# Two layers of cached attention and gated FFN on one core: one more K page kept between the layers, and the loads of layer 0 reordered

## The chip, the core and the metric

The program runs on one core of a Trainium2 chip. The engines that matter are TensorE (PE in the profile, its weight loads apart as PEld), VectorE (DVE), ScalarE (ACT) and SyncE (SP). SP issues every large load from device memory (HBM) into on-chip memory (SBUF); 16 DMA engines move it. The metric is the time of one execution in microseconds (us); lower is better.

## What is computed

One token of width 640 goes through attention, FFN, attention, FFN. Both attention layers use the same weights and the same caches, and so do both FFNs: a K page that layer 0 has read is the page that layer 1 needs. Attention looks at the last 4096 of 32768 cached positions, in 32 heads of width 192.

```python
def _A_ref(x, k_cache, v_cache, wq, wo):
    ...
    W = min(4096, max(256, Sk // 4))
    q = (x @ wq).reshape(B, Sq, Hq, Dh)          # then by head
    k = k_cache[:, :, Sk - W:, :]
    v = v_cache[:, :, Sk - W:, :]
    scores = einsum("bhqd,bhkd->bhqk", q, k) * (Dh ** -0.5)
    p = softmax(scores, axis=-1)
    o = einsum("bhqk,bhkd->bhqd", p, v)
    return o.reshape(B, Sq, Hq * Dh) @ wo

def _B_ref(x, w1, w3, w2):
    return einsum("bsf,fd->bsd", silu(x @ w1) * (x @ w3), w2)

x = A_x
x = x + _A_ref(_layernorm(x), ...)
x = x + _B_ref(_layernorm(x), ...)
x = x + _A_ref(_layernorm(x), ...)
x = x + _B_ref(_layernorm(x), ...)
```

The operands are bf16. One head's K (or V) for the window is 4096 x 192 values, 1.57 MB; wq is 7.9 MB, wo 7.9 MB, w1, w3 and w2 1.97 MB each.

## The kernel before

**Slots.** `arena` is a ring of `NSLOT = 16` slots in SBUF, each 128 partitions by `PGW = 6144` bf16 columns (1.57 MB). One K page, one V page or one fifth of wq fills a slot. wo comes in five units of nine chunks of 640 columns, plus a sixth unit of three chunks in a buffer of its own, `wo5`. w1 and w3 have 7680 columns: the first 6144 of each are the units `fa` and `fb`; their last 1536 each, with the first 2560 columns of w2, are the unit `fc`; the next 3200 columns of w2 are `fd`; the last 1920 of w2 stay for both layers in the buffer `keep`.

**One list of loads.** `loads` is built before anything runs and fixes the order of all loads: in each layer the five q units, then for each step i the V page of head number i − 6 (`LEAD` is 6) and the K page of head number i, then wo, then the FFN. `refill` (L191 to L205; its load is L203, that of the buffers without a slot L198) takes entries from the front as long as a slot is free. An entry that has no slot holds back all behind it. `done` frees a slot when its last reader has been recorded and calls `refill`. On the chip, SP executes the issues in that order, and each waits until the readers of the slot's former content have finished. It also waits for the load eight issues earlier, since loads take turns on eight semaphores.

**Kept pages.** K pages of the heads in `RETAIN` (14 of them) are not read again in layer 1. Thirteen stay in their slots from layer 0 to layer 1. The fourteenth, head 24 (`STASH`), is copied into PSUM and a small buffer and back by `stash`, so it holds no slot between. `ORDER` sets the order of the blocks of eight heads: heads 24 to 31, 16 to 23, 8 to 15, 0 to 7 in layer 0, and 8 to 15, 0 to 7, 16 to 23, 24 to 31 in layer 1. All of heads 0 to 7 are kept, so at the end of layer 0's attention thirteen slots are held and three are left for the stream. Layer 1's head 8, which is kept, comes first; its slot comes free when its products are done.

**Compute.** Every product is recorded through the helper `mm`, so all matmuls have line L80. A K page is turned by two transposes on DVE (L293) as it comes in, and then multiplied by twelve matmuls (`s_ps`); a kept page needs no second turning. Four heads share a softmax (L315 to L343). A V page takes 16 matmuls (`o_ps`). On PE the order of a step is V of head i − 6 first, then K of head i. After the last V come `combine`, `wo_proj` (18 matmuls for each wo unit), the sum into the residual (`y_to_residual`) and the layernorm; then `ffn`: 16 matmuls on `fa`, 16 on `fb`, 8 on `fc`, a short chain on ACT and DVE, and the w2 product, which frees `fc` and then `fd`. Layer 1 begins with another residual and layernorm, and `qproj` reads the five q units, 16 matmuls each. The tile `w` in the profile is the program's `w20`; `pss` holds the small PSUM results.

Of the kernel before, what the change touches and what calls it, by code (L numbers as in the profile page):

```python
# [17 lines left out]
NCH = 5  # L18
# [7 lines left out]
PGW = 6144  # L26
# [2 lines left out]

NSLOT = 16  # L30
STASH = 24
RETAIN = (0, 1, 2, 3, 4, 5, 6, 7, 8, 11, 14, 18, 21, 24)
MB = 2560
MN = 192
NSTASH = 2 * (3072 - MN)
LEAD = HB + 2
# [11 lines left out]
def kernel(  # L48
# [90 lines left out]
    keep = arn.tile([P, 1920], BF16, name="keep")  # L139
# [5 lines left out]
    loads = []  # L145

    wq_v = A_wq.rearrange("(p c) n -> c p n", c=NCH)
    wo_v = A_wo.rearrange("(b p e) n -> b p (e n)", b=H // HG, p=P, e=12)
    w1_v = B_w1.rearrange("(p c) n -> p (c n)", c=NCH)
    w3_v = B_w3.rearrange("(p c) n -> p (c n)", c=NCH)  # L150
    w2_v = B_w2.rearrange("(p f) n -> p (f n)", f=12)

    ORDER = ((3, 2, 1, 0), (1, 0, 2, 3))

    def head(layer, g):
        return HG * ORDER[layer][g // HG] + g % HG

    for layer in range(2):
        for c in range(NCH):
            loads.append((("q", layer, c), [(0, PGW, wq_v[c])]))  # L160
        for i in range(H + LEAD):
            for kind, g, cache in (("v", i - LEAD, A_v_cache), ("k", i, A_k_cache)):
                if not 0 <= g < H:
                    continue
                h = head(layer, g)
                if kind == "k" and layer == 1 and h in RETAIN:
                    if h == STASH:
                        loads.append((("k", 1, h), []))
                    continue
                loads.append(((kind, layer, h),  # L170
                              [(0, PGW, cache[0, h, S0:SK, :].rearrange("(p t) d -> p (t d)", p=P))]))
        for w in range(6):
            parts, ci, end = [], 9 * w, min(9 * w + 9, 48)
            while ci < end:
                to = min(end, ci - ci % 12 + 12)
                parts.append((640 * (ci - 9 * w), 640 * (to - ci),
                              wo_v[ORDER[layer][ci // 12]][:, 640 * (ci % 12):640 * (ci % 12 + to - ci)]))
                ci = to
            if w < 5:
                loads.append((("o", layer, w), parts))  # L180
            elif layer == 0:
                assert len(parts) == 1 and parts[0][1] == 1920
                loads.append((None, [(wo5[:], parts[0][2])]))
        loads.append((("fa", layer), [(0, PGW, w1_v[:, 0:PGW])]))
        loads.append((("fb", layer), [(0, PGW, w3_v[:, 0:PGW])]))
        loads.append((("fc", layer), [(0, 1536, w1_v[:, PGW:]), (1536, 1536, w3_v[:, PGW:]),
                                      (3072, 2560, w2_v[:, 0:2560])]))
        fd = [(0, 3200)] if layer == 0 else [(0, 1280), (1280, 1280), (2560, 640)]
        loads.append((("fd", layer), [(o, n, w2_v[:, 2560 + o:2560 + o + n]) for o, n in fd]))
        if layer == 0:  # L190
            loads.append((None, [(keep[:], w2_v[:, 5760:7680])]))  # L191

    def refill():
        while loads and (free or loads[0][0] is None):
# [20 lines left out]
    def page(key):  # L215
        return arena[:, home[key] * PGW:home[key] * PGW + PGW]

    def done(key):
        free.append(home.pop(key))
        refill()  # L220
# [59 lines left out]
    def k_source(layer, g):  # L280
        h = head(layer, g)
        fresh = layer == 0 or h not in RETAIN
        return ("k", layer if fresh or h == STASH else 0, h), fresh
# [11 lines left out]
    def k_page(layer, g, s_ps):  # L295
# [12 lines left out]
        if layer == 0 and h == STASH:  # L308
            stash(x, True)
            done(key)  # L310
        elif layer == 1 or h not in RETAIN:
            done(key)
# [70 lines left out]
    def y_open(name):  # L383

        y_ps = [ps_a.tile([P, 512], F32, tag="a", name=f"{name}{i}") for i in range(2)]
        for nh in range(2):
            for j in range(4):
                mm(y_ps[nh][32 * j:32 * j + 32, 0:320], lhsT=zero[:], rhs=ptm[:, 0:320],
                   start=True, stop=False, tile_position=(0, 32 * j))
        return y_ps  # L390

    def wo_proj(layer):
        y_ps = y_open("y_ps")
        for w in range(6):
            pg = page(("o", layer, w)) if w < 5 else wo5
            for cc in range(min(9, 48 - 9 * w)):
                ci = 9 * w + cc
                j = ci % 4
                for nh in range(2):
                    mm(y_ps[nh][32 * j:32 * j + 1, 0:320], lhsT=otd[:, ci:ci + 1],  # L400
                       rhs=pg[:, 640 * cc + 320 * nh:640 * cc + 320 * nh + 320],
                       start=False, stop=(ci >= 44), tile_position=(0, 32 * j))
            if w < 5:
                done(("o", layer, w))
        y_to_residual(y_ps)

    def w2_chunk(layer, fcx):
        if fcx >= 9:
            return keep, 640 * (fcx - 9)
        return (page(("fc", layer)), 3072 + 640 * fcx) if fcx < 4 else (page(("fd", layer)), 640 * (fcx - 4))  # L410

    def ffn(layer):
        if layer == 1:
            assert not loads
            spare = free[0] * PGW
            ident = arena[:, spare:spare + 256].bitcast(F32)
            nc.gpsimd.memset(ident, 0.0)
            nc.gpsimd.affine_select(out=ident, in_=ident, compare_op=ALU.not_equal, fill=1.0, base=0,
                                    pattern=[[-1, P]], channel_multiplier=1)
        g_ps = ps_a.tile([P, 512], F32, tag="a", name="g_ps")  # L420
        u_ps = ps_a.tile([P, 512], F32, tag="a", name="u_ps")
        for ps, kind, c0, c1, off in ((g_ps, "fa", 0, 4, 0), (u_ps, "fb", 0, 4, 0),
                                      (g_ps, "fc", 4, 5, 0), (u_ps, "fc", 4, 5, 1536)):
            pg = page((kind, layer))
            for c in range(c0, c1):
                for j in range(4):
                    mm(ps[32 * j:32 * j + 32, 0:384], lhsT=xs[:, c, 3:35],
                       rhs=_ap(pg, 0, P, off + 1536 * (c - c0) + 3 * j, [[12, 128], [1, 3]]),
                       start=(c == 0), stop=(c == NCH - 1), tile_position=(0, 32 * j))
            if kind != "fc":  # L430
                done((kind, layer))
        gu = w20.rearrange("p (g n) -> p g n", g=2)
        pin(nc.scalar.copy(out=gu[:, 0, :], in_=g_ps[:, 0:384]))
        pin(nc.vector.tensor_copy(out=gu[:, 1, :], in_=u_ps[:, 0:384]))
        gt_ps = m_ps[:, 0:24].rearrange("p (g k j) -> p g k j", g=2, k=3)
        for gi in range(2):
            for k in range(3):
                mm(gt_ps[:, gi, k, :], lhsT=gu[:, gi, k:384:3], rhs=sel4[:], start=True, stop=True)
        ex = sml.tile([P, 12], F32, tag="ex", name="ex")
        pin(nc.scalar.activation(out=ex[:], in_=gt_ps[:, 0, :, :].rearrange("p k j -> p (k j)"), func=ACTF.Exp,  # L440
                                 scale=-1.0))
        ut = sml.tile([P, 12], F32, tag="ut", name="ut")
        pin(nc.vector.tensor_copy(out=ut[:], in_=gt_ps[:, 1, :, :].rearrange("p k j -> p (k j)")))
        gut = sml.tile([P, 12], F32, tag="gut", name="gut")
        pin(nc.vector.tensor_tensor(out=gut[:], in0=gt_ps[:, 0, :, :].rearrange("p k j -> p (k j)"), in1=ut[:],
                                    op=ALU.mult))
        pin(nc.vector.tensor_scalar_add(out=ex[:], in0=ex[:], scalar1=1.0))
        pin(nc.vector.reciprocal(out=ex[:], in_=ex[:]))
        pin(nc.vector.tensor_tensor(out=_ap(htd[:], 0, P, 0, [[1, 3], [3, 4]]),
                                    in0=gut[:].rearrange("p (k j) -> p k j", k=3),  # L450
                                    in1=ex[:].rearrange("p (k j) -> p k j", k=3), op=ALU.mult))
        if layer == 1:
            return last_rows(ident)
        y_ps = y_open("y2_ps")
        for fcx in range(12):
            j = fcx % 4
            pg, off = w2_chunk(layer, fcx)
            for nh in range(2):
                mm(y_ps[nh][32 * j:32 * j + 1, 0:320], lhsT=htd[:, fcx:fcx + 1], rhs=pg[:, off + 320 * nh:off + 320 * nh + 320],
                   start=False, stop=(fcx >= 8), tile_position=(0, 32 * j))  # L460
            if fcx == 3:
                done(("fc", layer))
        done(("fd", layer))
        y_to_residual(y_ps)

    def last_rows(ident):
# [88 lines left out]
```

## Time and profile before

Three runs took 528.78, 528.95 and 529.55 us (median 528.95). The profiled execution has a span of 527.8 us, from its first to its last instruction.

| what | value |
|---|---|
| median of the runs | 528.95 us |
| span of the profiled execution | 527.8 us |
| PE busy, 2487 matmuls | 275.8 us (52%) |
| DVE busy | 256.5 us (49%) |
| ACT busy | 62.3 us (12%) |
| DMA, mean over the span | 421 GB/s, 221.97 MB |
| V pages loaded | 64 of 1536 KB |
| K pages loaded | 50 of 1536 KB |
| q units loaded | 10 of 1536 KB |

A name such as `arena<-in_A_v_cache_dram` says which tile is written from which tensor. In a list by time, the first number is the start within the span, the second how long it lasts; several instructions with small gaps are merged into one line with their count, and square brackets tell how long the engine sat idle before and what ended that. In a table by windows each line is a stretch of time with the busy time of each engine, the clock granted to PE, the busy share of the DMA engines and what they moved in GB/s.

### The profile page before, as it was taken

The numbers are of one execution on the slowest core, as the hardware profiler recorded it, in microseconds if no ns is written. First come the engines' busy times: TensorE is split into PE (matmuls) and PEld (weight loads), VectorE is DVE, ScalarE is ACT, GpSimd is POOL, SyncE is SP. The second block draws the span as 40 slices with busy tenths as digits, with TensorE's granted clock in tenths as the row PEclk, the third lists the DMA queues.
The fourth block names the chain that finished last, engine by engine and source line by source line (L and its number), as shares of the span: only waits on it lengthen the run. The fifth ranks groups of instructions, "written<-read, shape, count | busy, mean of one in ns | idle before, by whom it ended". The sixth has DMA issues, their size and how long they took to land.

```text
span 527.8 us, 6132 instructions
## 1 busy us (share of the span) xinstructions
PE 275.8 (52%) x2487; PEld 113.9 (22%) x2487; DVE 256.5 (49%) x393; ACT 62.3 (12%) x192; POOL 14.3 (3%) x66
## 2 busy tenths in 40 slices
PE   2354644463645555455445446678254655446545
PEld 1111212121212221122112212233121322112212
DVE  1199676656656475754001139431475654753001
ACT  1002020111102020102000002022111120202000
POOL 4000000000000000000000000000000000000000
PEclk9997968676766776586556557888677886586556
DMA  8999999999999999999999999999999999999995
GB/s 350 430 429 429 428 431 429 427 431 429 427 431 431 430 425 432 430 426 425 416 433 422 430 430 401 431 431 427 430 429 427 429 430 431 430 428 428 424 432 215
DMA packets 22356, 221.97 MB, mean 421 GB/s; under 512 B 2617, under 2 KB 2745, under 8 KB 5177
## 3 DMA queue, kind: packets, MB, share of 16 engines
q1 hardware_dynamic: 22184, 221.59, 99.1%
q8 instruction: 19, 0.31, 0.2%
q14 instruction: 9, 0.07, 0.0%
q10 hardware_dynamic: 144, 0.00, 0.0%
HBM read 221.58 MB, written 0.00 MB: 420 GB/s over the span
## 4 chain that ended last, share of the span: by engine, by line
DMA 86%; PE 6%; DVE 5%; ACT 1%; issue 1%; SPq 0%; DVEq 0%; ACTq 0%
DMA arena<-in_A_k_cache_dram 54%; DMA arena<-in_A_v_cache_dram 14%; DMA arena<-in_A_wo_dram 8%; DMA arena<-in_A_wq_dram 6%; DMA arena<-in_B_w_dram 5%; DVE arena L293 4%; PE s_ps L80 3%; PE o_ps L80 2%; PE y_ps L80 1%; SPq L203 0%; ACT w L330 0%; PE pss L80 0%; PE q_ps L80 0%; DVE t L315 0%; PE g_ps L80 0%
## 5 line engine op out<-in xcount | busy, mean ns | idle before, releaser
L80 PE MATMUL s_ps<-arena,wst 128*32 128x512 bf16 x768 | 155.2, 518 | 172.7 <-DVE arena L293 86.4
L293 DVE STREAM_TRANSPOSE arena<-arena 128x1536 uint32<-128x1536 uint32 x100 | 171.2, 1754 | 77.3 <-DMA arena<-in_A_k_cache_dram 77.0
L80 PE MATMUL o_ps<-arena,ptm 128*8 128x384 bf16 (+1 forms) x1024 | 116.7, 425 | 11.4 <-DMA arena<-in_A_v_cache_dram 11.3
L80 PEld LDWEIGHTS <-wst 128*32 128x32 bf16 x768 | 52.9, 115 | 257.9 <-issue 226.7
L80 PEld LDWEIGHTS <-ptm 128*8 128x8 bf16 (+1 forms) x1024 | 41.0, 100 | 49.0 <-issue 38.8
L325 ACT ACTIVATE tb<-m 32x16 f32<-32x16 f32 x16 | 3.4, 215 | 280.6 <-DVE m L322 280.6
L343 ACT COPY ptm<-w 32x64 bf16<-32x64 bf16 x80 | 23.6, 295 | 44.5 <-PE o_ps L80 41.4
L80 PE MATMUL y_ps<-arena,otd 128*1 128x320 bf16 x180 | 16.5, 448 | 15.0 <-DMA arena<-in_A_wo_dram 15.0
L80 PE MATMUL q_ps<-arena,xs 128*32 128x384 bf16 x160 | 14.5, 519 | 17.5 <-DMA arena<-in_A_wq_dram 14.9
L376 DVE SCALAR_TENSOR_TENSOR w<-pss,rl,mask 64x192 bf16<-64x192 f32 x16 | 6.7, 416 | 31.7 <-PE pss L80 31.7
L275 POOL COPY wst<-qt_sb 32x24 bf16<-32x24 bf16 x30 | 8.4, 281 | 434.4 <-PE s_ps L80 315.8
L333 DVE STREAM_TRANSPOSE w<-w 64x512 bf16<-64x512 bf16 x16 | 11.3, 705 | 14.4 <-ACT w L330 14.4
L241 DVE CAST w<-y_ps 128x320 bf16<-128x320 f32 x3 | 1.5, 492 | 33.8 <-PE y_ps L80 33.8
L315 DVE TENSOR_REDUCE t<-s_ps 64x1 f32<-64x512 f32 x16 | 10.6, 663 | 12.2 <-PE s_ps L80 12.1
L80 PEld LDWEIGHTS <-xs 128*32 128x32 bf16 x240 | 8.8, 125 | 35.1 <-issue 23.0
L268 DVE CAST qt_sb<-pss 32x192 bf16<-32x192 f32 x2 | 0.7, 345 | 30.9 <-PE pss L80 30.9
L343 DVE COPY ptm<-w 32x64 bf16<-32x64 bf16 x48 | 10.0, 208 | 11.7 <-PE o_ps L80 10.4
L348 DVE RECIPROCAL rl<-pss 64x1 f32<-64x1 f32 x16 | 2.6, 165 | 20.5 <-PE pss L80 20.4
L80 PEld LDWEIGHTS <-otd 128*1 128x1 bf16 x192 | 6.4, 102 | 25.2 <-issue 21.1
L330 ACT ACTIVATE w<-s_ps,nbt 64x512 bf16<-64x512 f32 x16 | 10.9, 682 | 5.6 <-DVE nbt L327 5.6
L369 ACT CAST w<-o_ps 128x384 bf16<-128x384 f32 x16 | 7.7, 478 | 31.7 <-PE o_ps L80 23.3
L80 PE MATMUL pss<-w,sel 128*64 128x192 bf16 x32 | 6.0, 273 | 9.5 <-ACT w L369 6.4
(81 smaller groups left out, 107.8 us busy)
## 6 DMA issues: line engine op xcount, KB each, us to landing
arena<-in_A_v_cache_dram SPq DMA_DIRECT2D x64, 1536.0 KB, 29.2
arena<-in_A_k_cache_dram SPq DMA_DIRECT2D x50, 1536.0 KB, 29.2
arena<-in_A_wq_dram SPq DMA_DIRECT2D x10, 1536.0 KB, 9.5
arena<-in_A_wo_dram SPq DMA_DIRECT2D x6, 1440.0 KB, 20.8
arena<-in_B_w_dram SPq DMA_DIRECT2D x4, 1536.0 KB, 10.9
arena<-in_A_wo_dram SPq DMA_DIRECT2D x4, 960.0 KB, 16.5
arena<-in_A_wo_dram SPq DMA_DIRECT2D x4, 480.0 KB, 15.0
arena<-in_B_w_dram SPq DMA_DIRECT2D x4, 384.0 KB, 14.8
```

The lines of the kernel that those rows point to most:

```text
L80: return pin(nc.tensor.matmul(*a, **k))
L241: pin(nc.vector.tensor_copy(out=y_sb[:, 320:640], in_=y_ps[1][:, 0:320]))
L275: pin((engs[a].copy if engs[a] is nc.scalar else engs[a].tensor_copy)(out=dst, in_=src))
L293: pin(nc.vector.transpose(x[:, w * sp:w * (sp + 1)].bitcast(U32), x[:, w * sp:w * (sp + 1)].bitcast(U32)))
L315: pin(nc.vector.reduce_max(out=t0[:, 0:1], in_=s_ps[0:64, :], axis=AX.X))
L325: pin(nc.scalar.mul(out=tb[32:64, :].rearrange("p (a z) -> p a z", a=4)[:, :, 0:HB], in_=mb, mul=-SCALE))
L330: pin(nc.scalar.activation(out=e[:], in_=s_ps[0:64, :], func=ACTF.Exp, bias=nbt[:, 0:1], scale=SCALE, accum_out=l[:]))
L333: pin(nc.vector.transpose(et[:], e[:]))
L343: pin((eng.copy if eng is nc.scalar else eng.tensor_copy)(out=dst, in_=src))
L348: pin(nc.vector.reciprocal(out=rl[half], in_=rl_ps[half]))
L369: pin(nc.scalar.copy(out=o_sb[:, 0:384], in_=o_ps[:, 0:384]))
L376: pin(nc.vector.scalar_tensor_tensor(out=om, in0=ot_ps[half], scalar=rl[half], in1=mask[half].unsqueeze(2).broadcast_to([64, 16, 12]), op0 ...
```

## The change

The list `RETAIN` gets head 9, so layer 1 loads 17 K pages instead of 18, and fourteen slots are held at the end of layer 0's attention instead of thirteen. In layer 0 each step's K page stands ahead of its V page in `loads`; the order of the products stays. In layer 0 the wo chunks 9, 10 and 11 are read last and from `wo5`, where chunks 45 to 47 were; layer 1's order is as before. Layer 1 reads `wo5` as layer 0 left it. Before, that was rows of block 0 (heads 0 to 7), where the reference has block 3 (heads 24 to 31) for layer 1's last three chunks; after the change it is block 3 in both layers. In layer 0's FFN `fc` holds the last 1536 columns of w1 and w3 alone, is loaded first and multiplied first; `fd` holds the first 5760 columns of w2. Layer 1's FFN is as before.

```diff
-RETAIN = (0, 1, 2, 3, 4, 5, 6, 7, 8, 11, 14, 18, 21, 24)
+RETAIN = (0, 1, 2, 3, 4, 5, 6, 7, 8, 9, 11, 14, 18, 21, 24)
...
+    def wo_order(layer):
+        last = ORDER[1][3]
+        kept = [12 * ORDER[layer].index(last) + e for e in (9, 10, 11)]
+        return [ci for ci in range(48) if ci not in kept] + kept
+
     for layer in range(2):
         for c in range(NCH):
             loads.append((("q", layer, c), [(0, PGW, wq_v[c])]))
         for i in range(H + LEAD):
-            for kind, g, cache in (("v", i - LEAD, A_v_cache), ("k", i, A_k_cache)):
+            pair = (("v", i - LEAD, A_v_cache), ("k", i, A_k_cache))
+            for kind, g, cache in pair[::-1] if layer == 0 else pair:
...
-            parts, ci, end = [], 9 * w, min(9 * w + 9, 48)
-            while ci < end:
-                to = min(end, ci - ci % 12 + 12)
-                parts.append((640 * (ci - 9 * w), 640 * (to - ci),
-                              wo_v[ORDER[layer][ci // 12]][:, 640 * (ci % 12):640 * (ci % 12 + to - ci)]))
-                ci = to
+            parts = []
+            for at, ci in enumerate(wo_order(layer)[9 * w:9 * w + 9]):
+                blk, e = ORDER[layer][ci // 12], ci % 12
+                if parts and parts[-1][2] == blk and parts[-1][3] + parts[-1][1] == e:
+                    parts[-1][1] += 1
+                else:
+                    parts.append([at, 1, blk, e])
+            parts = [(640 * at, 640 * n, wo_v[blk][:, 640 * e:640 * (e + n)]) for at, n, blk, e in parts]
...
-        loads.append((("fa", layer), [(0, PGW, w1_v[:, 0:PGW])]))
-        loads.append((("fb", layer), [(0, PGW, w3_v[:, 0:PGW])]))
-        loads.append((("fc", layer), [(0, 1536, w1_v[:, PGW:]), (1536, 1536, w3_v[:, PGW:]),
-                                      (3072, 2560, w2_v[:, 0:2560])]))
-        fd = [(0, 3200)] if layer == 0 else [(0, 1280), (1280, 1280), (2560, 640)]
-        loads.append((("fd", layer), [(o, n, w2_v[:, 2560 + o:2560 + o + n]) for o, n in fd]))
+        fa = (("fa", layer), [(0, PGW, w1_v[:, 0:PGW])])
+        fb = (("fb", layer), [(0, PGW, w3_v[:, 0:PGW])])
+        fc = [(0, 1536, w1_v[:, PGW:]), (1536, 1536, w3_v[:, PGW:])]
         if layer == 0:
-            loads.append((None, [(keep[:], w2_v[:, 5760:7680])]))
+            loads += [(("fc", 0), fc), fa, fb, (("fd", 0), [(0, 5760, w2_v[:, 0:5760])]),
+                      (None, [(keep[:], w2_v[:, 5760:7680])])]
+        else:
+            loads += [fa, fb, (("fc", 1), fc + [(3072, 2560, w2_v[:, 0:2560])]),
...
+        body = [(g_ps, "fa", 0, 4, 0), (u_ps, "fb", 0, 4, 0)]
+        rest_c = [(g_ps, "fc", 4, 5, 0), (u_ps, "fc", 4, 5, 1536)]
+        seq = rest_c + body if layer == 0 else body + rest_c
...
-            if kind != "fc":
+            if kind != "fc" or (layer == 0 and ps is u_ps):
                 done((kind, layer))
...
-            if fcx == 3:
-                done(("fc", layer))
-        done(("fd", layer))
+            if fcx == 8:
+                done(("fd", layer))
```

More of the change, by code (lines that the diff above doesn't have):

```diff
@@ L183 @@
                 loads.append((None, [(wo5[:], parts[0][2])]))
-        loads.append((("fa", layer), [(0, PGW, w1_v[:, 0:PGW])]))
-        loads.append((("fb", layer), [(0, PGW, w3_v[:, 0:PGW])]))
-        loads.append((("fc", layer), [(0, 1536, w1_v[:, PGW:]), (1536, 1536, w3_v[:, PGW:]),
-                                      (3072, 2560, w2_v[:, 0:2560])]))
-        fd = [(0, 3200)] if layer == 0 else [(0, 1280), (1280, 1280), (2560, 640)]
-        loads.append((("fd", layer), [(o, n, w2_v[:, 2560 + o:2560 + o + n]) for o, n in fd]))
-        if layer == 0:
-            loads.append((None, [(keep[:], w2_v[:, 5760:7680])]))
+        fa = (("fa", layer), [(0, PGW, w1_v[:, 0:PGW])])
+        fb = (("fb", layer), [(0, PGW, w3_v[:, 0:PGW])])
+        fc = [(0, 1536, w1_v[:, PGW:]), (1536, 1536, w3_v[:, PGW:])]
+        if layer == 0:
+            loads += [(("fc", 0), fc), fa, fb, (("fd", 0), [(0, 5760, w2_v[:, 0:5760])]),
+                      (None, [(keep[:], w2_v[:, 5760:7680])])]
+        else:
+            loads += [fa, fb, (("fc", 1), fc + [(3072, 2560, w2_v[:, 0:2560])]),
+                      (("fd", 1), [(o, n, w2_v[:, 2560 + o:2560 + o + n])
+                                   for o, n in ((0, 1280), (1280, 1280), (2560, 640))])]
     def refill():
@@ L395, in wo_proj @@
             pg = page(("o", layer, w)) if w < 5 else wo5
-            for cc in range(min(9, 48 - 9 * w)):
-                ci = 9 * w + cc
-                j = ci % 4
+            for cc, ci in enumerate(wo_order(layer)[9 * w:9 * w + 9]):
+                n = 9 * w + cc
+                j = n % 4
                 for nh in range(2):
@@ L401, in wo_proj @@
                        rhs=pg[:, 640 * cc + 320 * nh:640 * cc + 320 * nh + 320],
-                       start=False, stop=(ci >= 44), tile_position=(0, 32 * j))
+                       start=False, stop=(n >= 44), tile_position=(0, 32 * j))
             if w < 5:
@@ L409, in w2_chunk @@
             return keep, 640 * (fcx - 9)
-        return (page(("fc", layer)), 3072 + 640 * fcx) if fcx < 4 else (page(("fd", layer)), 640 * (fcx - 4))
+        if layer == 0:
+            return page(("fd", 0)), 640 * fcx
+        return (page(("fc", 1)), 3072 + 640 * fcx) if fcx < 4 else (page(("fd", 1)), 640 * (fcx - 4))
     def ffn(layer):
@@ L421, in ffn @@
         u_ps = ps_a.tile([P, 512], F32, tag="a", name="u_ps")
-        for ps, kind, c0, c1, off in ((g_ps, "fa", 0, 4, 0), (u_ps, "fb", 0, 4, 0),
-                                      (g_ps, "fc", 4, 5, 0), (u_ps, "fc", 4, 5, 1536)):
+        body = [(g_ps, "fa", 0, 4, 0), (u_ps, "fb", 0, 4, 0)]
+        rest_c = [(g_ps, "fc", 4, 5, 0), (u_ps, "fc", 4, 5, 1536)]
+        seq = rest_c + body if layer == 0 else body + rest_c
+        first, last = (4, 3) if layer == 0 else (0, 4)
+        for ps, kind, c0, c1, off in seq:
             pg = page((kind, layer))
@@ L428, in ffn @@
                        rhs=_ap(pg, 0, P, off + 1536 * (c - c0) + 3 * j, [[12, 128], [1, 3]]),
-                       start=(c == 0), stop=(c == NCH - 1), tile_position=(0, 32 * j))
-            if kind != "fc":
+                       start=(c == first), stop=(c == last), tile_position=(0, 32 * j))
+            if kind != "fc" or (layer == 0 and ps is u_ps):
                 done((kind, layer))
```

## The prediction

> **What bounds the kernel now.** I read the page from its span and DMA rows to the chain, then the answers by window and by time around the change of layers.
>
> ```profile
> span 527.8 us, 6132 instructions
> ...
> DMA  8999999999999999999999999999999999999995
> GB/s 350 430 429 429 428 431 429 427 431 429 427 431 431 430 425 432 430 426 425 416 433 422 430 430 401 431 431 427 430 429 427 429 430 431 430 428 428 424 432 215
> ...
> DMA 86%; PE 6%; DVE 5%; ACT 1%; issue 1%; SPq 0%; DVEq 0%; ACTq 0%
> ```
>
> The chain that ended last is 86% DMA, and outside the first and last slice the DMA engines move about 430 GB/s. So the time now is bytes over rate. A page of 1.573 MB at 430 GB/s takes 3.66 us, and SP's issues of K and V pages come every 3.65 us (41.03, 44.66, 48.30). Whatever bytes go away are gained, and whatever leaves the engines without an issued load is lost, one for one.
>
> What has to be known is therefore how far SP runs ahead where slots are few. Here are SP's issues around the end of layer 0's attention, and PE's readings of V pages there (start, duration, in brackets the idle time before and what ended it):
>
> ```profile
> 242.50 7.00 SPq L203 DMA_DIRECT2D arena<-in_A_v_cache_dram  x3
> 251.31 13.98 SPq L203 DMA_DIRECT2D arena<-in_A_wo_dram  x7
> ...
> 268.40 13.03 SPq L203 DMA_DIRECT2D arena<-in_B_w_dram  x6
> ...
> 284.58 15.02 SPq L203 DMA_DIRECT2D arena<-in_A_wq_dram  x5
> ```
>
> ```profile
> 249.82 1.45 PE L80 MATMUL o_ps<-arena,ptm 128*8 128x384 bf16 x16 [0.70 <-DMA arena<-in_A_v_cache_dram]
> 253.47 1.45 PE L80 MATMUL o_ps<-arena,ptm 128*8 128x384 bf16 x16 [2.19 <-DMA arena<-in_A_v_cache_dram]
> 257.37 1.45 PE L80 MATMUL o_ps<-arena,ptm 128*8 128x384 bf16 x16 [2.45 <-DMA arena<-in_A_v_cache_dram]
> ```
>
> PE waits for V, not the reverse, and a reading that ends at 251.27 lets SP issue at 251.31, 0.04 us later. With three slots each freed slot has two other transfers, 7.3 us, ahead of it. The table by windows shows that this is enough (columns: length, engines, granted PE clock, DMA share, GB/s):
>
> ```profile
> 200.00:246.00 46.00, 25.48 (x190) 10.36 (x189) 26.35 (x38) 5.31 (x17) 0.56 (x2) 0.66 1.01 429
> 246.00:312.00 66.00, 32.05 (x356) 13.11 (x356) 6.63 (x24) 4.46 (x15) 0.01 (x1) 0.55 1.01 425
> 312.00:330.00 18.00, 11.73 (x61) 4.28 (x62) 16.66 (x21) 3.32 (x11) 0.83 (x3) 0.69 1.01 412
> ```
>
> 425 GB/s in the narrow stretch, against 429 ahead of it: almost nothing is lost there now.
>
> **What the change takes away.** One K page of layer 1 (head 9): 1.573 MB, −3.66 us of a stream that does not pause. With it go two DVE transposes of 1.75 us and an issue of 0.33 us, both beside the stream and worth nothing. The FFN of layer 0 is issued in six loads instead of seven, same bytes; wo in seven, as before. No matmul is added or removed; the new orders of K and V, of the wo chunks and of w1, w3 and w2 move loads on SP's one queue and cost nothing by themselves. That K comes ahead of V delays a V page by one transfer, 3.66 us, early in layer 0, where eight loads are in flight and PE is idle half the time; it also brings the last K page one transfer earlier, so that its softmax chain (6.2 us from the last K product at 241.4 to the first product of V page 28 at 247.66) ends ahead of the V pages that need it. I take nothing for either.
>
> **What it adds: two slots instead of three.** From the last K page of layer 0 to the release of head 8 and 9 in layer 1 only one other slot covers a freed one. Call p the transfer (3.66 for a page) and S what lies between SP's issue and the reader's start beyond p when nothing is queued ahead. The trace has one such start, the first loads:
>
> ```profile
> 0.74 2.52 SPq L203 DMA_DIRECT2D arena<-in_A_wq_dram  x5
> ...
> 14.29 1.47 PE L80 MATMUL q_ps<-arena,xs 128*32 128x384 bf16 x16 [2.09 <-DMA arena<-in_A_wq_dram]
> 17.94 1.47 PE L80 MATMUL q_ps<-arena,xs 128*32 128x384 bf16 x16 [2.18 <-DMA arena<-in_A_wq_dram]
> ```
>
> The third page, back to back with the first, is read at 14.29: 14.29 − 0.74 − 3 × 3.66 = 2.57; the fourth at 17.94 gives 2.56. I take S = 2.6 (about 2.0 to the stream, 0.6 from its end to PE). From below: the 1.2 KB output, issued at 525.08, is waited for until 525.74 + 1.0 = 526.74, so S is not under 1.66. From above: the V page issued at 242.50 is read at 249.82, 7.32 − 3.66 = 3.66, though part of that was queueing. The value is nearest the first-load row, as that is the same kind of load from a standstill.
>
> A page read at once then blocks its slot for S + 1.47 + 0.04 = 4.11 us beyond its transfer, and the other slot's transfer covers 3.66: 0.45 us idle; since both slots then shift, only every second page pays. Going through the list in this way (R: a slot's release; the load's data begins 2.0 later or when the former ends), idle time arises at:
>
> - V page 27 (of head number 27 in layer 0's order; units by their number): 0.46. V page 28: 0.56, as V 26 is read on PE behind K 31's twelve products (2.75 us as in 316.77). V 30 and wo unit 0: 0.46 each. Together 1.94.
> - wo units: a unit is 3.43 us, its reading 1.75, so the block is 4.40. Unit 1 0.23, unit 2 0.74 (4.40 − 3.43 − 0.23), unit 3 0.23, unit 4 0.16 (its predecessor lands in two parts and only twelve products are left). Together 1.36.
> - `fa` waits for unit 4's reading: 4.40 less `wo5` (1.14) and `fc` (1.83): 1.43. `fb` waits for `fc`'s reading, which comes after the residual and layernorm (3.48 us, from 276.38 to 279.86) and its own eight products (1.05): 1.47. `fd`, `keep`, q0 and q1 are covered. Together 2.90.
> - q2 waits for q0's reading, behind the next residual and layernorm: 1.08. q4: 0.46. Together 1.54.
> - K of head 12 waits for q4: 0.46. K of head 13 waits for head 8's kept page, thus for the chain from the last q product to the K weights (2.3 us, 310.41 to 312.72) and twelve products (2.75): 1.39. Together 1.85. Head 9's slot comes 2.75 later and the stream has caught up.
>
> Sum: 1.94 + 1.36 + 2.90 + 1.54 + 1.85 = 9.6 us idle. Net 9.6 − 3.66 = +5.9 us: 533.7 against the span of 527.8. The median of the runs is 1.15 us above that span, so 534.9 us.
>
> With S = 1.66 the same walk leaves 3.1 us idle, net −0.5; with S = 3.66 it leaves 19.3, but the walk of the kernel before would then lose 1.5 as well: net +14.1. In the Trainium skill, "DMA: Bandwidth & Descriptors", section "Anatomy of one DMA — SWDGE (gpsimd) path", a load costs a fixed 2.0 us or so plus bytes at 436 GB/s, measured on another issue path than this one. The first loads show 2.6; by 2.0 the walk gives 4.9 idle and a net of +1.3, and the sum here doesn't use it.
>
> The readings of 1.45 to 1.75 us are those of PE at the clock of this stretch, granted 0.55 in the mean, 0.50 in most 2 us windows. At full clock a V page takes 0.85 (16 products at 242.53). PE is busy about half the time here and would be idle a little more, so I keep the slow durations. All at full speed, the walk with S = 2.6 leaves 2.6 us idle.
>
> **The rivals.**
>
> A, the forecast: two slots leave gaps at every second load and at four chains. 534.9.
>
> B, the gap is longer in mid-stream than at the start. For: the one place where SP runs late now, 319.52 (issue of the V page after K 13), lies in the stretch with 412 GB/s (312 to 330), that is 18 us × 18 / 430 = 0.75 us lost where the walk gives none; if all of that is the late start, S is 2.6 + 0.75 = 3.35. Against: turning and products run there too. At S = 3.3 the loss grows by 5.4 us (0.7 of the 1.06 between the sums for 2.6 and 3.66, 5.9 and 14.1): 540.3.
>
> C, the other side: PE runs at full clock in this stretch. Readings then take 0.85 to 1.0, a page blocks its slot for 2.6 + 0.87 + 0.04 = 3.5, less than the 3.66 that cover it, and only the chains pay: 2.6 − 3.66 = −1.05, 527.9. It decides as soon as readings fall under 1.0 us. For: single windows at 264 and 286 are granted 0.9 and more. Against: the q and V readings here all take 1.45 to 1.47. The Trainium skill, "TensorE: Matmul & The Clock Gate", section "Part 1: The HAM clock gate", has the gate open only after some 3.4 us of sustained work and close again after an idle window. By that rule C does not come; the readings of 1.45 us with 2.2 us of idle ahead agree.
>
> D, a load starts as fast as the small output write: S = 1.66, −0.5, 528.5.
>
> E, the stream is not held at all, because the reordering hides everything: −3.66, 525.3. Against: the walk has all of the reordering in it.
>
> That the change doesn't load less can't be: the page is no longer in the list.
>
> **How the numbers follow.** A 0.62, B 0.14, C 0.11, D 0.09, E 0.04. A measurement of this kernel tells 0.2%, about 1.1 us, from no change. C stands on that bound: 0.07 of it faster, 0.04 the same. With E and 0.02 of D, faster is 0.13; with the rest of D the same is 0.11. A and B are slower: 0.76. The range leaves out E, and B's far end: from D's 528.5 to 542, a little short of the upper end of S (543). The forecast's own range is 532 to 538, S from 2.2 to 2.95.
>
> **What would show it.** K loads fall from 50 to 49 and MB from 221.97 to 220.4. SP's waits on `y_ps`, `q_ps`, `o_ps` and `g_ps` in place of DMA waits; GB/s of 385 or so between 235 and 325 (90 us with 9.6 idle) where it was 425; the two largest dips at `fa` and `fb`, then K of head 13 and q2; V and q readings still at 1.45 us. If the dips lie at the chains alone, C or D holds; if each load of the stretch comes 4.2 us or more after the one before, B. I am wrong if GB/s in the stretch stays above 420, or if time goes outside it.

## The result

The changed kernel takes 550.21 us (547.83 to 552.59 in six runs) beside 529.1 us for the kernel before (528.75 to 529.55 in six runs): ratio 1.0404, 95% interval 1.0384 to 1.0425. It was forecast slower, at 534.9 us with 542 as the upper end; it is slower by 21 us instead of 6.

The page of the changed kernel, its span, its DMA rows and its chain:

```profile
span 548.4 us, 6126 instructions
...
DMA  8999999999999999999898988999999999999995
GB/s 353 430 429 429 428 429 429 430 430 428 429 428 430 430 426 430 429 361 336 306 337 295 357 305 333 423 430 428 429 429 428 428 430 429 430 429 429 426 428 233
DMA packets 22067, 220.39 MB, mean 402 GB/s; under 512 B 2584, under 2 KB 2712, under 8 KB 4888
...
DMA 89%; PE 8%; DVE 1%; issue 0%; ACT 0%; SPq 0%; ACTq 0%
```

The bytes are down by the one K page, 221.97 to 220.39 MB, and outside slices 18 to 25 the rate is what it was. In those eight slices (of 13.7 us each) it is 295 to 361 GB/s. The row of busy shares hardly shows it, with 8s and 9s. It adds up how long packets take, and packets take longer here: those of 12 KB take 0.46 us on average between 100 and 200 and 0.52 us between 230 and 345, where one in fourteen takes over 0.8 us. Here is the stretch as one window and what follows it, first the kernel before, then the changed kernel, as one window and by stages (length, engines, granted PE clock, DMA share, GB/s):

```profile
230.00:345.00 115.00, 62.23 (x580) 25.08 (x580) 38.34 (x73) 11.14 (x35) 1.40 (x5) 0.64 1.01 424
345.00:500.00 155.00, 86.41 (x814) 36.64 (x809) 75.39 (x125) 23.01 (x71) 3.31 (x12) 0.73 1.01 429
```

```profile
230.00:345.00 115.00, 49.00 (x477) 20.38 (x474) 22.35 (x51) 6.50 (x20) 0.83 (x3) 0.55 0.90 333
...
230.00:263.00 33.00, 13.29 (x127) 5.32 (x128) 7.56 (x16) 2.93 (x9) 0.00 (x0) 0.60 0.93 353
263.00:287.00 24.00, 10.11 (x115) 3.78 (x109) 0.92 (x2) 0.48 (x1) 0.00 (x0) 0.50 0.90 325
287.00:305.00 18.00, 6.82 (x74) 2.96 (x69) 2.89 (x12) 1.49 (x5) 0.00 (x0) 0.50 0.87 304
305.00:331.00 26.00, 8.71 (x98) 4.15 (x97) 1.50 (x6) 0.83 (x3) 0.00 (x0) 0.50 0.88 329
331.00:345.00 14.00, 10.07 (x76) 4.18 (x75) 9.48 (x15) 0.77 (x2) 0.83 (x3) 0.67 0.90 343
345.00:500.00 155.00, 92.39 (x794) 37.98 (x795) 83.37 (x136) 24.45 (x77) 3.86 (x14) 0.74 1.01 429
```

A stage's loss is its length times the share of 430 GB/s that is missing:

| stage | forecast, us idle | measured, us lost |
|---|---|---|
| last V pages (230 to 263) | 1.94 | 5.9 |
| wo (263 to 287) | 1.36 | 5.9 |
| FFN of layer 0 (287 to 305) | 2.90 | 5.3 |
| wq of layer 1 (305 to 331) | 1.54 | 6.1 |
| first K pages of layer 1 (331 to 345) | 1.85 | 2.8 |
| sum | 9.6 | 26.0 |

Before, the same stretch lost 6 / 430 × 115 = 1.6 us. 26.0 − 1.6 − 3.66 for the page = 20.7, and the spans differ by 548.4 − 527.8 = 20.6. So all of the time went here, and the excess over the forecast, 16.4 us, lies in every stage: 4.0 to 4.6 us in those of V, wo and wq, where there are many loads and hardly a chain, 2.4 in the FFN and 1.0 in the first K pages.

Two loads show it: SP's issues and PE's readings of the same V pages and q units.

```profile
254.34 0.33 SPq L213 DMA_DIRECT2D arena<-in_A_v_cache_dram  x1
...
322.11 0.33 SPq L213 DMA_DIRECT2D arena<-in_A_wq_dram  x1
```

```profile
252.84 1.45 PE L80 MATMUL o_ps<-arena,ptm 128*8 128x384 bf16 x16 [2.81 <-DMA arena<-in_A_v_cache_dram]
258.23 1.45 PE L80 MATMUL o_ps<-arena,ptm 128*8 128x384 bf16 x16 [3.93 <-DMA arena<-in_A_v_cache_dram]
262.76 1.45 PE L80 MATMUL o_ps<-arena,ptm 128*8 128x384 bf16 x16 [3.09 <-DMA arena<-in_A_v_cache_dram]
...
320.59 1.47 PE L80 MATMUL q_ps<-arena,xs 128*32 128x384 bf16 x16 [4.12 <-DMA arena<-in_A_wq_dram]
324.87 1.47 PE L80 MATMUL q_ps<-arena,xs 128*32 128x384 bf16 x16 [2.80 <-DMA arena<-in_A_wq_dram]
330.99 1.47 PE L80 MATMUL q_ps<-arena,xs 128*32 128x384 bf16 x16 [4.65 <-DMA arena<-in_A_wq_dram]
```

The V page issued at 254.34 is read at 262.76: 8.42 us, less the transfer of 3.66 leaves 4.76. The q unit issued at 322.11 is read at 330.99: 8.88 − 3.66 = 5.22. The forecast took 2.6 for this. PE waits 2.8 to 4.65 us for each of the loads shown.

### The profile page after: what moved, and what is told of

Same layout as the page of the kernel before. It is cut to its first block, busy times and chain, and to the rows that moved or that the text cites. A ratio compares the mean times of both kernels' runs of the same rounds, so it can differ in the third digit from the quotient of the medians.

```text
span 548.4 us, 6126 instructions
## 1 busy us (share of the span) xinstructions
PE 282.0 (51%) x2487; PEld 111.7 (20%) x2487; DVE 252.9 (46%) x391; ACT 62.3 (11%) x192; POOL 14.3 (3%) x66
## 2 busy tenths in 40 slices
DMA packets 22067, 220.39 MB, mean 402 GB/s; under 512 B 2584, under 2 KB 2712, under 8 KB 4888
## 4 chain that ended last, share of the span: by engine, by line
DMA 89%; PE 8%; DVE 1%; issue 0%; ACT 0%; SPq 0%; ACTq 0%
DMA arena<-in_A_v_cache_dram 48%; DMA arena<-in_A_k_cache_dram 20%; DMA arena<-in_A_wo_dram 10%; DMA arena<-in_B_w_dram 7%; DMA arena<-in_A_wq_dram 5%; PE s_ps L80 3%; PE o_ps L80 2%; PE y_ps L80 1%; DVE arena L303 1%; PE q_ps L80 1%; PE u_ps L80 0%; PE g_ps L80 0%; PE f_ps L80 0%; SPq L213 0%; PE pss L80 0%
## 5 line engine op out<-in xcount | busy, mean ns | idle before, releaser
L303 DVE STREAM_TRANSPOSE arena<-arena 128x1536 uint32<-128x1536 uint32 x98 | 167.9, 1754 | 64.5 <-DMA arena<-in_A_k_cache_dram 64.3
L80 PE MATMUL o_ps<-arena,ptm 128*8 128x384 bf16 (+1 forms) x1024 | 101.1, 450 | 88.3 <-DMA arena<-in_A_v_cache_dram 88.3
L80 PEld LDWEIGHTS <-ptm 128*8 128x8 bf16 (+1 forms) x1024 | 35.4, 104 | 134.2 <-issue 104.7
L80 PE MATMUL y_ps<-arena,otd 128*1 128x320 bf16 x180 | 16.9, 459 | 20.6 <-DMA arena<-in_A_wo_dram 20.6
```

Source lines behind the costliest of these rows:

```text
L80: return pin(nc.tensor.matmul(*a, **k))
L303: pin(nc.vector.transpose(x[:, w * sp:w * (sp + 1)].bitcast(U32), x[:, w * sp:w * (sp + 1)].bitcast(U32)))
```

## The experiments

**Is it the slots or the reorderings?** Two kernels undo one side each.

The changed kernel with head 9 not kept (three slots, reorderings kept):

```diff
-RETAIN = (0, 1, 2, 3, 4, 5, 6, 7, 8, 9, 11, 14, 18, 21, 24)
+RETAIN = (0, 1, 2, 3, 4, 5, 6, 7, 8, 11, 14, 18, 21, 24)
```

> The changed kernel with head 9 taken out of the kept pages again: three free slots, all reorderings of layer 0 kept. Theory 1 (two free slots can't cover a load's start of some 4.5 us plus the reading of 1.5 us; three can): the stream is full again, 528 to 532 us. Rival R1 (the reorderings of K and V, wo and FFN cost the time): 545 us or more.

Measured 529.04 us, ratio to before 0.9999 (0.9989 to 1.0008). The stretch:

```profile
230.00:345.00 115.00, 61.86 (x585) 25.49 (x583) 36.86 (x72) 11.14 (x35) 1.39 (x5) 0.60 1.01 424
```

The kernel before with head 9 kept (two slots, nothing reordered):

```diff
-RETAIN = (0, 1, 2, 3, 4, 5, 6, 7, 8, 11, 14, 18, 21, 24)
+RETAIN = (0, 1, 2, 3, 4, 5, 6, 7, 8, 9, 11, 14, 18, 21, 24)
```

> The kernel before with head 9 kept and nothing reordered: two free slots. Theory 1: as slow as the changed kernel or slower, 550 to 560 us, since the reorderings only shorten the chains. Rival R1: about 525 us, one page less to load and no loss.

Measured 547.19 us, ratio 1.0336 (1.0304 to 1.0368). The stretch:

```profile
230.00:345.00 115.00, 50.58 (x478) 20.59 (x477) 25.09 (x55) 8.07 (x25) 0.84 (x3) 0.58 0.91 344
```

The fifteenth page costs 18 us by itself, and the reorderings cost and gain nothing where three slots are free. Rival R1 falls. That the plain kernel is no slower than the changed one is a miss of theory 1's detail: the reorderings don't shorten the stretch with two slots either.

**One slot: the start of a load into an empty queue.** The changed kernel with head 10 kept too:

```diff
-RETAIN = (0, 1, 2, 3, 4, 5, 6, 7, 8, 9, 11, 14, 18, 21, 24)
+RETAIN = (0, 1, 2, 3, 4, 5, 6, 7, 8, 9, 10, 11, 14, 18, 21, 24)
```

> The changed kernel with head 10 kept as well: one free slot, so that each load is issued into an idle queue. It measures the start S alone: a V page's issue to issue is S + 3.66 + 1.5. If S is 4.5 us whatever else runs (theory 1a): 9.7 us from V issue to V issue, 640 us or so in all. If S is 2.6 into an idle queue and grows only while another load runs (theory 1b): 7.8 us, about 600 us.

Measured 608.08 us, ratio 1.1497 (1.1474 to 1.1520). An issue, the readings around it, and a window over three V pages:

```profile
269.42 0.33 SPq L213 DMA_DIRECT2D arena<-in_A_v_cache_dram  x1
```

```profile
260.15 1.47 PE L80 MATMUL o_ps<-arena,ptm 128*32 128x384 bf16 x16 [4.37 <-DMA arena<-in_A_v_cache_dram]
267.93 1.45 PE L80 MATMUL o_ps<-arena,ptm 128*8 128x384 bf16 x16 [6.30 <-DMA arena<-in_A_v_cache_dram]
275.58 1.45 PE L80 MATMUL o_ps<-arena,ptm 128*8 128x384 bf16 x16 [6.21 <-DMA arena<-in_A_v_cache_dram]
```

```profile
259.70:283.10 23.40, 4.37 (x48) 1.61 (x49) 0.00 (x0) 0.00 (x0) 0.00 (x0) 0.50 0.55 202
```

275.58 − 269.42 − 3.66 = 2.50: into an empty queue the start is what the first loads of the program had shown, and V pages follow each other in 7.65 to 7.78 us, as 3.66 + 2.6 + 1.5 has it. So the forecast's value was right for a load alone and wrong for most loads issued while another runs: 1b, not 1a.

The trace also holds, for each load, sixteen packets of 4 bytes, one for each DMA engine, which come when that engine's share is done. The times for four loads of the changed kernel (q units 1 to 4) and four of the one-slot run, first, twelfth and last of sixteen:

```
changed:   312.20  313.59  314.66 | 317.15  317.79  320.21 | 321.74  322.87  324.47 | 327.34  327.74  330.65
one slot:  259.03  259.48  259.82 | 266.92  267.32  267.55 | 274.70  275.09  275.20 | 282.28  282.66  282.93
```

The readings at 315.00, 320.59, 324.87 and 330.99 come 0.34 to 0.40 us after the last of the sixteen, as that at 275.58 does (0.38). So the reader waits for the slowest engine. In these four loads of the one-slot run all sixteen are done within 0.5 to 0.8 us, in those of the changed kernel the last comes 2.5 to 3.3 us after the first. Of the q unit issued at 322.11, twelve engines are done at 327.74; had all been, its start would have been 327.74 + 0.34 − 322.11 − 3.66 = 2.3. The same sum gives 2.5 and 3.1 for the q units issued at 311.98 and 316.51. In these loads, then, most engines are nearly as early as in a load alone, and what is late is the shares of a few.

Each of these packets counts the load's semaphore up by one, and the trace has the times of that too, so that loads which overlap can be told apart. From the first to the sixteenth count, median over the loads that end between 240 and 330, it takes 0.7 us with one slot, 2.1 in the changed kernel and 2.0 in the kernel before. There the engines are as far out of step, but two more loads are queued and nobody waits. In the Trainium skill, "DMA: Bandwidth & Descriptors", section "Why a DMA increments its semaphore by 16 and not by 1", a load runs on up to 16 engines that finish independently, and only the full count means that all has landed; the sixteen packets and the readings agree.

**More loads in flight, same bytes.** Loads cut into halves by columns, each of which waits for the readers of its own half:

```diff
-                              [(0, PGW, cache[0, h, S0:SK, :].rearrange("(p t) d -> p (t d)", p=P))]))
+                src = cache[0, h, S0:SK, :].rearrange("(p t) d -> p (t d)", p=P)
+                cut = PGW // 2 if (layer == 0 and i >= H - 1) or (layer == 1 and i < LEAD) else PGW
+                loads.append(((kind, layer, h), [(at, cut, src[:, at:at + cut]) for at in range(0, PGW, cut)]))
...
+            fa = (("fa", 0), [(0, 3072, w1_v[:, 0:3072]), (3072, 3072, w1_v[:, 3072:PGW])])
+            fb = (("fb", 0), [(0, 3072, w3_v[:, 0:3072]), (3072, 3072, w3_v[:, 3072:PGW])])
...
```

What the lines shown leave out: wq units are halved too, wo units are cut after the fifth chunk and `fd` after 3200 columns.

> The changed kernel with every load between layer 0's last K page and layer 1's first K pages cut into two loads of half the columns, each of which waits for the readers of its own half (layer 1's wq halves hold the columns that PE reads first). Same bytes, same slots, four loads in flight instead of two. Theory 1 (a fixed start per load, hidden by the number of loads in flight): the loss of some 24 us falls to under 8, 526 to 534 us. Rival R3 (the rate with two pages' worth of bytes in flight is what is low, whatever their number): no better than 545 us.

Measured 535.14 us, ratio 1.0115 (1.0100 to 1.0130). The stretch:

```profile
230.00:345.00 115.00, 61.18 (x552) 22.29 (x550) 31.09 (x62) 9.57 (x30) 0.84 (x3) 0.59 0.99 391
```

333 GB/s in the changed kernel, 391 here, with the same two slots: a loss of 10.4 us instead of 25.9. R3 falls. The expected span of results was 526 to 534, so a little more is left than theory 1 gave.

The same halves with head 9 not kept, as a control:

```diff
-RETAIN = (0, 1, 2, 3, 4, 5, 6, 7, 8, 9, 11, 14, 18, 21, 24)
+RETAIN = (0, 1, 2, 3, 4, 5, 6, 7, 8, 11, 14, 18, 21, 24)
```

> The half loads with head 9 taken out of the kept pages: three slots, the stream should be full with whole loads already. If halving a load costs nothing by itself (theory 1): 528 to 530 us. If the smaller loads (descriptors of half the length, twice the issues) cost rate, part of what is left in the half-load run is theirs: 531 us or more.

Measured 531.16 us, ratio 1.0039 (1.0024 to 1.0053), the stretch at 420 GB/s where the kernel before has 424. Halves aren't free: they cost about 2 us with three slots, and if they cost the same with two, that much of what is left in the half-load run is theirs.

Quarters for V, K, w1 and w3, two or three chunks for wo:

```diff
-                cut = PGW // 2 if (layer == 0 and i >= H - 1) or (layer == 1 and i < LEAD) else PGW
+                cut = PGW // 4 if (layer == 0 and i >= H - 1) or (layer == 1 and i < LEAD) else PGW
...
```

> As the kernel with half loads, but V pages 25 to 31, K 31, layer 1's first K pages and w1 and w3 in quarters, wo in pieces of two or three chunks; wq stays in halves. If what is left of the loss with half loads (about 10 us) is starts, it shrinks: 530 to 533 us. If it is the chains between stages (combine, residual and layernorm twice, q to the K weights), nothing changes: 534 to 537 us, or worse through more issues.

Measured 534.39 us, ratio 1.0097 (1.0080 to 1.0114): inside the second range, 0.75 us better than halves with runs that overlap. Most of its loss, 6.2 of 9.9 us (393 GB/s over 230 to 345), sits at two chains, the residual and layernorm ahead of `fa` (280 to 292) and q to the K weights (318 to 330):

```profile
280.00:292.00 12.00, 6.22 (x61) 2.53 (x61) 1.91 (x9) 1.06 (x4) 0.00 (x0) 0.64 0.81 298
...
318.00:330.00 12.00, 7.95 (x48) 3.35 (x48) 9.95 (x18) 1.52 (x5) 0.84 (x3) 0.75 0.89 341
```

Then the quarters with the load of `keep` ahead of `fa`:

```diff
-            loads += [(("fc", 0), fc), fa, fb, (("fd", 0), [(0, 3200, w2_v[:, 0:3200]), (3200, 2560, w2_v[:, 3200:5760])]),
-                      (None, [(keep[:], w2_v[:, 5760:7680])])]
+            loads += [(("fc", 0), fc), (None, [(keep[:], w2_v[:, 5760:7680])]), fa, fb,
+                      (("fd", 0), [(0, 3200, w2_v[:, 0:3200]), (3200, 2560, w2_v[:, 3200:5760])])]
```

> The quarter loads with the load of w2's kept rows (no slot, 1.14 us) moved from behind fd to ahead of fa, where both slots wait for the residual and layernorm. If chains are what is left: up to 1.1 us less there, some given back ahead of q0: 533 to 534.4 us. If starts are: no change, 534.4 us.

Measured 534.29 us, ratio 1.0095 (1.0075 to 1.0114). Inconclusive: its time can't be told from the quarters alone. At the chain itself (280 to 292) the rate is 342 GB/s instead of 298, 1.2 us less lost, and the whole stretch has 391 instead of 393, so what is won there is lost again elsewhere.

**Two half loads in one slot.** The half loads with head 10 kept too:

```diff
-RETAIN = (0, 1, 2, 3, 4, 5, 6, 7, 8, 9, 11, 14, 18, 21, 24)
+RETAIN = (0, 1, 2, 3, 4, 5, 6, 7, 8, 9, 10, 11, 14, 18, 21, 24)
```

> The half loads with head 10 kept as well: one free slot, so two loads of 0.79 MB take turns in it where the one-slot run had one of 1.57 MB. If the late start comes with a second load in flight, whatever its size (theory 1b): a half is blocked for 1.83 + 4.4 + 0.75 = 7.0 us, V page to V page 7 us, about 595 us in all. If every start is 2.5 us: 5.1 us from V page to V page, 565 us or so.

Measured 577.18 us, ratio 1.0907 (1.0886 to 1.0929), between the two. First halves of V pages are read at:

```profile
250.18 0.83 PE L80 MATMUL o_ps<-arena,ptm 128*32 128x384 bf16 x8 [0.62 <-DMA arena<-in_A_v_cache_dram]
...
255.24 0.81 PE L80 MATMUL o_ps<-arena,ptm 128*8 128x384 bf16 x8 [2.38 <-DMA arena<-in_A_v_cache_dram]
...
260.65 0.81 PE L80 MATMUL o_ps<-arena,ptm 128*8 128x384 bf16 x8 [2.33 <-DMA arena<-in_A_v_cache_dram]
...
267.24 0.81 PE L80 MATMUL o_ps<-arena,ptm 128*8 128x384 bf16 x8 [2.73 <-DMA arena<-in_A_v_cache_dram]
```

They are 5.7 us apart in the mean, which gives a start of 5.7 − 1.83 − 0.85 = 3.0 us, but they differ. The one read at 255.24 has a start of 5.06 − 2.68 = 2.4, and its sixteen counts come within 0.3 us; that read at 267.24 has 6.59 − 2.68 = 3.9, with fifteen counts within 0.4 us and the last 1.95 after the first. Both had the other half in flight. So a second load in flight has no fixed price: of these two, the start is long where one engine is late.

**A second queue.** Every second load of the stretch from ACT's queue:

```diff
+            narrow = (key[:2] in (("o", 0), ("fa", 0), ("fb", 0), ("fd", 0), ("q", 1))
+                      or (key[:2] == ("v", 0) and 1 <= key[2] < HG) or (key[:2] == ("k", 1) and HG <= key[2] < 2 * HG))
+            turn[0] ^= narrow
+            eng = nc.scalar if narrow and turn[0] else nc.sync
             for off, n, src in parts:
-                pin(nc.sync.dma_start(out=arena[:, s * PGW + off:s * PGW + off + n], in_=src))
+                pin(eng.dma_start(out=arena[:, s * PGW + off:s * PGW + off + n], in_=src))
```

> The changed kernel with every second load of the narrow stretch (V of layer 0 from the last K page on, wo, w1 to w2 of layer 0, layer 1's wq and first K pages) issued from ACT's queue instead of SP's. Theory 2a (a load that is issued while another runs starts late because both stand in one queue): its start falls to the 2.5 us that the one-slot run showed, 533 to 538 us. Theory 2b (the lateness is of the 16 DMA engines, which get out of step and of which the slowest sets the landing): no gain, 546 to 552 us.

Measured 548.64 us, ratio 1.0353 (1.0318 to 1.0388). PE's readings of V pages 29 to 31 come in a pair:

```profile
253.38 1.45 PE L80 MATMUL o_ps<-arena,ptm 128*8 128x384 bf16 x16 [2.34 <-DMA arena<-in_A_v_cache_dram]
260.68 1.45 PE L80 MATMUL o_ps<-arena,ptm 128*8 128x384 bf16 x16 [5.84 <-DMA arena<-in_A_v_cache_dram]
263.37 1.45 PE L80 MATMUL o_ps<-arena,ptm 128*8 128x384 bf16 x16 [1.24 <-DMA arena<-in_A_v_cache_dram]
```

263.37 − 253.38 = 10.0 us for two pages, 5.0 each, no better than with one queue. The page read at 260.68 was issued by SP at 251.08. Thirteen of its engines are done by 256.98, which would be a start of 2.6 us, the last three at 258.13, 258.39 and 260.29. ACT's load, issued at 254.88, moves its packets from 256.5 on, so again single engines are late, and nothing clear of the noise is won: 2b. It isn't a clean refutation of 2a, since the late engines now also have the other queue's packets to move.

**Half of the reading.** Half of the matmuls left out that read the stretch's V, wo, w1, w3 and wq, as the expectation says:

```diff
-            for c2 in range(4):
+            for c2 in (0, 3) if layer == 1 else range(4):
...
-        for mq in range(4):
+        for mq in (0, 3) if layer == 0 and g >= 26 else range(4):
...
+                if layer == 0 and w < 5 and cc % 2:
+                    continue
...
-            for c in range(c0, c1):
+            for c in (0, 3) if layer == 0 and c0 == 0 else range(c0, c1):
```

> The changed kernel with half of the matmuls left out that read V pages 26 to 31, wo units 0 to 4, w1 and w3's first 6144 columns of layer 0 and wq of layer 1 (so the output is not the reference's). A reading takes 0.75 us instead of 1.47. Theory 1 (a slot is blocked for start plus reading, two slots share it): each of some 17 loads comes 0.37 us earlier, 543 to 546 us. Rival R2 (PE's slow clock in this stretch makes the loss): 535 us or less. If the reading doesn't count at all: 549 to 552 us.

Measured 545.92 us, ratio 1.0310 (1.0270 to 1.0350), 4.3 us under the changed kernel. A reading of a V page is now:

```profile
256.01 0.81 PE L80 MATMUL o_ps<-arena,ptm 128*8 128x384 bf16 x8 [2.84 <-DMA arena<-in_A_v_cache_dram]
```

That is 0.81 us instead of 1.45, and one reading of all 16 products at a faster clock took 0.82 in the changed kernel (at 243.14). The wo units' readings didn't get shorter (the first takes 1.76 us with 10 products as with 18), so the run halves those of V, w1, w3 and wq alone. Shorter readings count as start plus reading has it, and PE's clock is not what makes most of the loss: R2 falls.

**K ahead of V.** The changed kernel without it:

```diff
-            for kind, g, cache in pair[::-1] if layer == 0 else pair:
+            for kind, g, cache in pair:
```

> The changed kernel with V ahead of K in layer 0 again, all else kept. The kernel before with head 9 kept and nothing else took 547.2 us, so one of the reorderings costs about 3 us. If it is K ahead of V (it puts V 26's reading behind the last K page's products): 545 to 547 us. If it is the FFN's or wo's new order: 549 to 552 us.

Measured 548.09 us (545.98 to 551.21), ratio 1.0362 (1.0322 to 1.0402). Inconclusive: with 550.21 (547.83 to 552.59) for the changed kernel and 547.19 (544.01 to 548.29) for the plain one, which reordering costs something, if any does, stays open.

## Why the prediction was wrong

**What bounds the kernel** was right. The stream sets the time, one page less is 3.66 us less, and each gap counts in full: 26.0 − 1.6 − 3.66 gives the difference of the spans to 0.1 us. **That nothing else moves** was right too: the rate after 345 is 429 GB/s in both kernels, and at three slots the reorderings are worth nothing (0.9999).

**Two slots instead of three** was the right place and the right mechanism. The start plus the reading blocks a slot longer than the other slot's transfer covers: the plain fifteenth page costs 18 us, halving the reading gives 4.3 us back, four loads in flight instead of two give 15 us back.

**The step that failed is the value of S.** "I take S = 2.6", from the first loads of the program, as "the same kind of load from a standstill". The standstill was the error. A load into an empty queue does start in 2.5 us, as the one-slot run shows, but with two slots a load is issued while the other runs, and then it is 4.76 and 5.22 us in the two shown above. Three more agree: the V page issued at 250.07 and read at 258.23 gives 4.50, the q units issued at 311.98 and 316.51 and read at 320.59 and 324.87 give 4.95 and 4.70. The prediction's S is for a load with "nothing queued ahead", and for the V pages part of the surplus can be waiting behind the other load: when that of 254.34 was issued, the one ahead was still to be read, at 258.23. The runs don't divide it. In the q unit issued at 322.11 all of it is four late engines.

The size follows from there. The prediction's own sums are 9.6 us idle for S of 2.6 and 19.3 for 3.66; carried on in a straight line, the measured loss of 26.0 belongs to an S of 4.4, an estimate. And the trace of the kernel before had the surplus: the sixteen counts of its first loads lie within 0.6 us, those of its loads between 240 and 330 2.0 us apart. Adding the 1.4 us between them to 2.6 gives an S of 4.0, an estimate too. Of the bound of 3.66 from above the text said that part of it was queueing; it came from a stretch with three slots and was no bound for one with two.

**"Only every second page pays"** is the same sum, S + 1.51 − 3.66 for two pages: 0.45 us with S at 2.6, but 2.35 to 3.05 with 4.5 to 5.2, so 1.2 to 1.5 us a load. **The chains** at `fa`, `fb`, q2 and K of head 13 were named rightly, and the quarter loads, where the single starts are mostly hidden, still lose there: (430 − 298) / 430 × 12 = 3.7 us and (430 − 341) / 430 × 12 = 2.5 us.

**The rivals.** B was the right direction, a start longer in mid-stream, and was priced too low (S of 3.35, 540.3 us). Its evidence, the 412 GB/s after an issue late at 319.52, may have been that same effect; no run tells. C did not come, as forecast: readings stayed at 1.45 to 1.47 us at a granted clock of 0.50, but for one of 0.82 us at 243.14. D is refuted by the one-slot run (2.50, not 1.66), E by the loss.

**What would show it.** MB came out at 220.39 as said and K loads at 49. The rate of 385 GB/s between 235 and 325 was too high: it is 327 there. SP does wait for PE (`o_ps` 10.7 us between 226 and 345), but not in place of DMA (V pages 27.5). "4.2 us or more after the one before" was the mark set for B, and the readings of V and q bear it. Neither of the two signs named for being wrong came: both were for a loss that is missing or elsewhere, not for one of another size.

What stays open is why single DMA engines fall behind. For the full stream the trace points at one cause. The engines also move the program's instructions, in packets of 16384 bytes that take 0.9 us or so. In the kernel before they are this queue (packets, MB, share of the engines' time):

```profile
q8 instruction: 19, 0.31, 0.2%
```

Such packets start at 29.10, 282.70 and 298.40 there, and in the first load that ends after each of them is through one engine is 1.1, 1.1 and 0.8 us later against the others than in the load ahead, and about as late in the loads behind. No run takes these packets away, so this is not shown, and in the changed kernel three of them between 230 and 345 (255.98, 293.42, 312.35) are too few for the late engines of nearly every load. The second queue didn't cure it, though that test is confounded. No kernel that keeps the fifteenth page came under the kernel before; the best, 534.3 us, is 1% above it.

## What to carry to other kernels

Before a buffer is given away, ask how many loads the stream still has in flight there, and price the start of a load as it is in a running stream, from issue to reader, not at the program's first load: here 2.5 us alone and 4.5 to 5.2 beside another page. A full stream hides how far its engines are out of step, so look there at when each load's engines finish before its slack is given away. If buffers must be few, cut the loads and let each piece wait for its own reader: pieces in flight, not bytes, hide the start (333 to 391 GB/s with the same two slots). One page saved is worth 3.66 us, once; a gap of about 1 us at each of more than 20 loads costs more.

## What the runs showed of the hardware

The sixteen DMA engines that share a load don't stay in step. In four V pages that ran alone their shares ended 0.5 to 0.8 us apart. In the kernel before the first loads end within 0.6 us, those between 240 and 330 2.0 us apart (median), where three slots hide it. In the changed kernel's q units it was 2.5 to 3.3 us, and there the reader and the next issue wait for the last engine. Rates by what is in flight, from the windows above, readings and chains included: one page 202 GB/s, two pages 333, four halves 391, three pages 424. A DMA busy share of 0.87 to 0.93 stood beside a rate of 71% to 82% of the full one, so in such a stretch the rate is to be read and not the share.
